# Attention in an fp32 kernel: the factors of the states' softmax go from a diagonal matrix onto the softmax matrix itself

## The chip, the cores and the metric

The kernel runs on one core of a Trainium2 chip. The metric is device time in microseconds (us), the median of several executions. One further execution was recorded by the hardware profiler, with each instruction's start and length on TensorE (PE; its weight loads are PEld), VectorE (DVE), ScalarE (ACT), GpSimd (POOL) and the DMA queues; SyncE (SP) issues most of the DMAs.

## The reference

Three stages follow one another: an attention between 512 tokens and 32 states for each of 4 batches and 8 heads, a dense layer with the mish activation, and a layer in which each token goes through one of 8 experts. Only the attention is edited:

```python
scores = scale * np.matmul(x, state.transpose(0, 1, 3, 2))      # B, H, 512, 32
a = np.exp(scores - scores.max(-1, keepdims=True))
a /= a.sum(-1, keepdims=True) + 1e-09
xread = np.matmul(a, state)
scores2 = scale * np.matmul(state, x.transpose(0, 1, 3, 2))     # B, H, 32, 512
a2 = np.exp(scores2 - scores2.max(-1, keepdims=True))
a2 /= a2.sum(-1, keepdims=True) + 1e-09
sread = np.matmul(a2, x)
out = np.concatenate([xread, sread], axis=2)                    # then the dense layer and the experts
```

## The kernel before

**Attention.** The function `attention` works in eight units, two per batch, each with four heads, so that 4 x 32 states fill the 128 partitions. Unit `u` passes four steps, one loop round apart: in round `t` the program writes `s1(t)`, `s2(t - 1)`, `s3(t - 2)` and `s4(t - 3)`.

- `s1` turns the tokens (`xt`, evacuated as `xT`), multiplies with the states (`sc`) and copies the scores out (`ss`).
- `s2` makes both softmaxes. The one over the states goes over GpSimd: `a` is the score minus its maximum `mx` (L336), ScalarE's exponential, and the product with the reciprocals `sm` (L351). For the one over the tokens TensorE turns the scores (`sb`), VectorE takes the maximum `mb`, ScalarE writes the exponential `a2` and its sums `sbs` in one instruction (L346), and VectorE makes the reciprocals of `sbs` (L353). These are one factor per row of `a2`. L355 spreads them on the diagonal of a 128 x 128 matrix, `dg`.
- `s3` turns `a` with four plain turns (`at`, L368) and brings `a2` to its turned form `a2t` by four fp32 matmuls with `dg` (L366), which apply the factors on the way; ScalarE copies `a2t` out as `a2T` (L371).
- `s4` multiplies the tokens with `a2T` (`sr`, L385); VectorE copies the result out (`XS`).

**Beside it.** From the first round on, `convert_w` turns the weights of the dense layer, 32 pieces that arrive in a 64-bit format, into pairs of reduced-precision matrices (`wih` and `wil`, `woh` and `wol`). Each piece passes GpSimd (L100), ScalarE (L97, L74), VectorE twice (L71) and GpSimd again (L75). Only two raw pieces fit (`w`), so the next load waits for a conversion.

**Dense layer.** For chunk `c` of 512 tokens and slice `f` of 128 hidden units `product` gives `m`, which is split into `mh` and `ml`; `l1` gives `h`; `mish_a` and `mish_b` are ScalarE and VectorE work on `h`; `g_split` gives `gh` and `gl`; `l2` adds into `acc`. Every product is three matmuls (`mm3`, L106 to L108). `split_x` splits the attention's result into `xh` and `xl`, for one half of a chunk with GpSimd (L75). The first rounds of the dense layer already run in the attention's last rounds.

**Experts.** A plan on VectorE and TensorE (`po`, L649) gives `perm`; with it GpSimd gathers tiles of tokens (`xg`, L884), TensorE turns them (`gt`, L889), multiplies with two weight matrices (`hp`, then, after a turn `ht` at L915, `y`), and GpSimd scatters the result (`ys`).

**The order.** No order is written out for all this up to the last tiles of the experts. A scheduler sorts the instructions of each engine from its own estimates of how long each takes, within the data dependences and the buffers. The changed program was scheduled anew.

The lines the change touches in `s3`:

```python
if n:
    T.matmul(o[:, js], d[key][:, js], d["dg"], start=True, stop=True)
else:
    T.transpose(o[:, js], d[key][:, js], ident)
```

Of the kernel before, what the change touches and what calls it, by code (L numbers as in the profile page):

```python
# [8 lines left out]
F32 = mybir.dt.float32  # L9
# [6 lines left out]
ALU = mybir.AluOpType  # L16
# [5 lines left out]
P = 128  # L22
# [30 lines left out]
def body(tc, x, state, w_in, w_out, ee, tau, w1, w2, out):  # L53
    nc = tc.nc
    T, V, A, G, Y = nc.tensor, nc.vector, nc.scalar, nc.gpsimd, nc.sync
    stack = ExitStack()

    def pool(name, bufs=1, **kw):
        return tc.tile_pool(name=name, bufs=bufs, **kw)

    def tsc(o, i, s1, op0, s2=None, op1=None):
        if op1 is None:
            V.tensor_scalar(out=o, in0=i, scalar1=s1, scalar2=None, op0=op0)  # L63
        else:
            V.tensor_scalar(out=o, in0=i, scalar1=s1, scalar2=s2, op0=op0, op1=op1)
# [7 lines left out]
    def split(hi, lo, src, eng=None):  # L73
        A.activation(hi, src, AF.Copy)  # L74
        (eng or V).tensor_tensor(out=lo, in0=src, in1=hi.bitcast(F32), op=ALU.subtract)  # L75
# [34 lines left out]
    with stack:  # L110
# [16 lines left out]
        ident = const.tile([P, P], F32, name="ident")  # L127
# [110 lines left out]
        def f32r(n, i, name):  # L238

            return xpool.tile([P, 512], F32R, tag=f"x{n}{i}", name=name)  # L240
# [25 lines left out]
        def attention(meanwhile):  # L266
            pa = ExitStack()
            tmp = pa.enter_context(pool("pa"))
# [21 lines left out]
            for h in range(4):  # L290
                q, r = divmod(h, 2)
                hs = slice(h * NST, (h + 1) * NST)
                o = SBD[hs, :, q, r * D : (r + 1) * D]
# [34 lines left out]
            def s2(u):  # L328
                d = ns[u]
                ss = d["ss"]  # L330
                v = ss.rearrange("p (g n) -> p g n", n=NST)
                mx = tmp.tile([P, 16], F32, tag="mx", bufs=2, name=f"mx{u}")
                V.tensor_reduce(mx, v, axis=AX, op=ALU.max)
                a = tmp.tile([P, 512], F32, tag="a", bufs=2, name=f"a{u}")
                av = a.rearrange("p (g n) -> p g n", n=NST)
                G.tensor_tensor(out=av, in0=v, in1=mx.unsqueeze(2).to_broadcast([P, 16, NST]), op=ALU.subtract)  # L336
                o = ps.tile([P, 512], F32, tag="acc", bufs=4, name=f"sb{u}")
                for j in range(KT):
                    T.transpose(o[:, j * P : (j + 1) * P], ss[:, j * P : (j + 1) * P], ident)
                A.activation(a, a, AF.Exp, scale=SCALE)  # L340
                mb = tmp.tile([P, 1], F32, tag="mb", bufs=2, name=f"mb{u}")
                V.tensor_reduce(mb, o, axis=AX, op=ALU.max)
                tsc(mb, mb, -SCALE, ALU.mult)
                a2 = tmp.tile([P, 512], F32, tag="a2", bufs=2, name=f"a2{u}")
                sb = tmp.tile([P, 1], F32, tag="sb", bufs=2, name=f"sbs{u}")
                A.activation(a2, o, AF.Exp, scale=SCALE, bias=mb, accum_out=sb)  # L346
                sm = tmp.tile([P, 16], F32, tag="sm", bufs=2, name=f"sm{u}")
                V.tensor_reduce(sm, av, axis=AX, op=ALU.add)
                tsc(sm, sm, 1e-9, ALU.add)
                V.reciprocal(sm, sm)  # L350
                G.tensor_tensor(out=av, in0=av, in1=sm.unsqueeze(2).to_broadcast([P, 16, NST]), op=ALU.mult)  # L351
                tsc(sb, sb, 1e-9, ALU.add)
                V.reciprocal(sb, sb)  # L353
                dg = tmp.tile([P, P], F32, tag="dg", bufs=2, name=f"dg{u}")
                tsc(dg, ident, sb, ALU.mult)  # L355
                d.update(a=a, a2=a2, dg=dg)

            def s3(u):
                d = ns[u]
                for n, key in enumerate(("a", "a2")):  # L360
                    o = ps.tile([P, 512], F32, tag="acc", bufs=4, name=f"{key}t{u}")
                    for j in range(KT):
                        js = slice(j * P, (j + 1) * P)
                        if n:

                            T.matmul(o[:, js], d[key][:, js], d["dg"], start=True, stop=True)  # L366
                        else:
                            T.transpose(o[:, js], d[key][:, js], ident)  # L368
                    if n:
                        t = d["a2T"] = tmp.tile([P, 512], F32, tag="a2T", bufs=2, name=f"a2T{u}")  # L370
                        A.activation(t, o, AF.Copy)  # L371
                    else:
                        if u < 2:
                            xh[0, u], xl[0, u] = f32r("h", u, f"xh0{u}"), f32r("l", u, f"xl0{u}")
                            split(xh[0, u], xl[0, u], o)
                        A.activation(AT[u // 2][:, u % 2, :], o, AF.Copy)
# [21 lines left out]
            for t in range(NU + 3):  # L398
                if t == 4:
                    load(3)  # L400
                if t < NU:
                    s1(t)
                if 0 <= t - 1 < NU:
                    s2(t - 1)
                if 0 <= t - 2 < NU:
                    s3(t - 2)
                if 0 <= t - 3 < NU:
                    s4(t - 3)
                for _ in range(t > 0):
                    if len(order) > len(order0) - FIRST:  # L410
                        convert_w()
                if t == 4:
                    embeddings(tmp)
                meanwhile(t)
# [725 lines left out]
```

## Time and profile before

| | us |
|---|---|
| timed runs: median of 3 (lowest, highest) | 734.07 (734.06, 740.17) |
| the profiled execution | 730.14 |
| its span, first to last instruction | 728.4 |

A profile shows one execution. A row of a timeline has the start and the length of an instruction or of several alike ones, the engine, the line of the kernel, what was written from what, and in square brackets the engine's idle time ahead of it with the releaser. Starts are counted from the start of the span. [...] Matmuls overlap, so the spacing of their starts tells more than their lengths.

### The profile page before, as it was taken

Reading aid. Unit: us, or ns where it says so; the run is one execution under the profiler, and the core shown is the slowest. Engines: PE = TensorE matmul, PEld = TensorE weight load, DVE = VectorE, ACT = ScalarE, POOL = GpSimd, SP = SyncE. Lnnn points to the kernel's source line nnn. Section 1 sums busy time; section 2 is a strip of 40 time slices with the busy share of each in tenths; the row PEclk is TensorE's granted clock in tenths of the full one; section 3 lists DMA queues with packets and bytes.
Section 4 is the critical chain, followed back from the end, with each engine's and each line's share of the span. In section 5 each row is a group of like instructions: output and inputs, shape, how many; then the busy total and the mean of one; then the engine's idle time right before and its main releaser. Section 6 shows DMA issues by size and latency. Waiting matters only on the chain.

```text
span 728.4 us, 11317 instructions
## 1 busy us (share of the span) xinstructions
PE 693.2 (95%) x3681; PEld 581.1 (80%) x3681; DVE 476.0 (65%) x981; ACT 452.6 (62%) x782; POOL 194.3 (27%) x165
## 2 busy tenths in 40 slices
PE   8888989899999999999999988799999999999994
PEld 8788868788888888888887867677888888888883
DVE  5987899998576865665667984573444752257741
ACT  5876988888697777666776776613434641246640
POOL 2785455462000210300002264212111312123101
PEclk9999999999999999999999999799999999999999
DMA  8552142340010100001000167304415631257530
GB/s 196 153 160 88 59 144 91 126 145 16 1 58 0 59 1 1 0 1 59 15 0 1 50 195 223 113 30 174 153 51 180 249 132 58 76 197 251 191 133 17
DMA packets 45499, 70.12 MB, mean 96 GB/s; under 512 B 23402, under 2 KB 23402, under 8 KB 45428
## 3 DMA queue, kind: packets, MB, share of 16 engines
q1 hardware_dynamic: 42068, 59.29, 25.3%
q0 software_dynamic: 3360, 9.99, 4.2%
q8 instruction: 31, 0.51, 0.3%
q14 instruction: 40, 0.33, 0.1%
HBM read 60.33 MB, written 9.98 MB: 97 GB/s over the span
## 4 chain that ended last, share of the span: by engine, by line
PE 45%; issue 25%; DMA 12%; DVE 9%; ACT 4%; POOL 3%; SPq 2%; POOLq 0%; DVEq 0%; ACTq 0%
DMA out<-ys,ix 7%; PE acc L106 7%; PE acc L107 7%; PE acc L108 7%; PE h L106 4%; PE h L107 4%; PE h L108 4%; DMA es<-in_moe_w 2%; DMA w<-in_moe_w_in 2%; PE m L106 2%; PE m L107 2%; PE m L108 2%; PE lg L557 1%; SPq L285 1%; PE y L108 1%
## 5 line engine op out<-in xcount | busy, mean ns | idle before, releaser
L106 PE MATMUL acc<-woh,gh 128*128 128x512 f32 x272 | 109.2, 406 | 2.3 <-ACT gh L74 2.2
L107 PE MATMUL acc<-wol,gh 128*128 128x512 f32 x272 | 109.5, 404 | 0.0
L108 PE MATMUL acc<-woh,gl 128*128 128x512 f32 x272 | 96.1, 400 | 0.0
L931 POOL DMA_INDIRECT out<-ys,ix x21 | 21.1, 1007 | 194.7 <-DVE ys L63 187.2
L477 DVE TENSOR_TENSOR er<-er 128x512 f32<-128x512 f32 x68 | 53.3, 784 | 29.1 <-ACT er L475 29.0
L106 PE MATMUL y<-w2h,hth 128*128 128x512 f32 x168 | 68.0, 404 | 0.8 <-ACTq L872 0.8
L106 PE MATMUL hp<-w1h,xth 128*128 128x512 f32 x168 | 68.5, 408 | 0.0
L475 ACT ACTIVATE er<-h,mb__103 128x512 f32<-128x512 f32 x68 | 46.5, 684 | 34.0 <-PE h L108 32.0
L108 PE MATMUL hp<-w1h,xtl 128*128 128x512 f32 x168 | 66.9, 399 | 0.0
L107 PE MATMUL hp<-w1l,xth 128*128 128x512 f32 x168 | 66.8, 398 | 0.0
L107 PE MATMUL y<-w2l,hth 128*128 128x512 f32 x168 | 66.5, 396 | 0.4 <-DVEq L872 0.4
L108 PE MATMUL y<-w2h,htl 128*128 128x512 f32 x168 | 66.7, 397 | 0.0
L106 PEld LDWEIGHTS acc<-woh,gh 128*128 128x128 f32 x272 | 52.0, 192 | 14.4 <-ACT gh L74 2.8
L74 ACT ACTIVATE hth<-ht 128x512 fp32r<-128x512 f32 x42 | 23.0, 595 | 64.3 <-PE ht L915 61.2
L107 PEld LDWEIGHTS acc<-wol,gh 128*128 128x128 f32 x272 | 52.3, 192 | 11.2
L108 PEld LDWEIGHTS acc<-woh,gl 128*128 128x128 f32 x272 | 51.2, 190 | 11.9 <-DVE gl L75 0.5
L74 ACT ACTIVATE xth<-gt 128x512 fp32r<-128x512 f32 x21 | 12.4, 595 | 75.2 <-PE gt L889 75.2
L500 ACT ACTIVATE h<-er,mb__103 128x512 f32<-128x512 f32 x68 | 47.1, 694 | 12.6 <-DVE er L477 10.4
L107 PE MATMUL h<-xl,mh 128*128 128x512 f32 x128 | 50.5, 395 | 2.5 <-POOL xl L75 2.5
L106 PE MATMUL h<-xh,mh 128*128 128x512 f32 x128 | 51.1, 399 | 0.0
L108 PE MATMUL h<-xh,ml 128*128 128x512 f32 x128 | 50.3, 393 | 0.0
L501 ACT ACTIVATE er<-er,mb__103 128x512 f32<-128x512 f32 x68 | 49.2, 723 | 1.4
(434 smaller groups left out, 1689.7 us busy)
## 6 DMA issues: line engine op xcount, KB each, us to landing
sg<-in_moe_w SPq DMA_DIRECT2D x48, 512.0 KB
w<-in_moe_w_in SPq DMA_DIRECT2D x16, 512.0 KB, 3.9
w<-in_moe_w_out SPq DMA_DIRECT2D x16, 512.0 KB, 3.2
es<-in_moe_w SPq DMA_DIRECT2D x32, 256.0 KB, 3.3
xn<-in_x SPq DMA_DIRECT2D x32, 128.0 KB, 3.6
x1d<-x SPq DMA_DIRECT2D x13, 256.0 KB, 3.3
x1d<-part SPq DMA_DIRECT2D x4, 256.0 KB
xg<-x1d,perm POOLq DMA_INDIRECT x21, 4.4
```

The costliest lines, as they stand in the source:

```text
L74: A.activation(hi, src, AF.Copy)
L106: T.matmul(o, lh, rh, start=first, stop=False)
L107: T.matmul(o, lh, rl, start=False, stop=False)
L108: T.matmul(o, ll, rh, start=False, stop=last)
L285: Y.dma_start(XN[b][:, g, :, r * D : (r + 1) * D], src[g, r])
L475: A.activation(z, h, AF.Tanh, scale=0.5, bias=mb_[:, 0:1])
L477: V.tensor_tensor(out=z, in0=z, in1=z, op=ALU.mult)
L500: A.activation(r, z, AF.Square, scale=QS, bias=mb_[:, 1:2])
L501: A.activation(z, z, AF.Square, scale=QS, bias=mb_[:, 2:3])
L557: T.matmul(o[:, j], xt[:, k * P : (k + 1) * P], enT[:, k, :].unsqueeze(1).to_broadcast([P, 8, NE]), start=k == 0, stop=k == KT - 1)
L931: G.indirect_dma_start(out=out[:, :], out_offset=bass.IndirectOffsetOnAxis(ap=ix, axis=0), in_=y, in_offset=None, bounds_check=NTOK - 1, o ...
```

## The change

The reciprocals of the sums are no longer put on a diagonal. VectorE multiplies them, one factor per row, onto the exponential `a2` in place (128 x 512 instead of 128 x 128 elements), and `a2` is turned as `a` is, by four plain turns. The tile `dg` goes; all other lines stay.

```diff
@@ s2
                 tsc(sb, sb, 1e-9, ALU.add)
                 V.reciprocal(sb, sb)
-                dg = tmp.tile([P, P], F32, tag="dg", bufs=2, name=f"dg{u}")
-                tsc(dg, ident, sb, ALU.mult)
-                d.update(a=a, a2=a2, dg=dg)
+                tsc(a2, a2, sb, ALU.mult)
+                d.update(a=a, a2=a2)
@@ s3
                     for j in range(KT):
                         js = slice(j * P, (j + 1) * P)
-                        if n:
-
-                            T.matmul(o[:, js], d[key][:, js], d["dg"], start=True, stop=True)
-                        else:
-                            T.transpose(o[:, js], d[key][:, js], ident)
+                        T.transpose(o[:, js], d[key][:, js], ident)
```

Since the program is scheduled anew, instructions also change places. Lines behind L354 have a number lower by one, behind L366 by five in the changed program. In the rows below, the number after a name is that of a buffer.

VectorE in the sixth unit, with the row that makes `dg`, before:

```order
L63 TENSOR_SCALAR sbs_804<-sbs_804 128x1
L63 TENSOR_SCALAR sm_806<-sm_806 128x16
L353 RECIPROCAL sbs_804<-sbs_804 128x1
L350 RECIPROCAL sm_806<-sm_806 128x16
L63 TENSOR_SCALAR dg_813<-ident,sbs_804 128x128
L71 SCALAR_TENSOR_TENSOR wc07x<-wc07x,w_846 128x512
```

and in the changed program, where `a_798` is the exponential `a2` of this unit:

```order
L63 TENSOR_SCALAR sbs_799<-sbs_799 128x1
L63 TENSOR_SCALAR sm_801<-sm_801 128x16
L353 RECIPROCAL sbs_799<-sbs_799 128x1
L350 RECIPROCAL sm_801<-sm_801 128x16
L63 TENSOR_SCALAR a_798<-a_798,sbs_799 128x512
L333 TENSOR_REDUCE mx_867<-ss_783 128x16
```

The scaling stands where `dg` was made; behind it the next unit's maximum now comes ahead of the weight conversion.

GpSimd at the end of the dense layer's first chunk, where it converts weights and splits the attention's result for chunk 1 (`xl`), before:

```order
L75 TENSOR_TENSOR wol_1105<-wc17x,woh_1104 128x512
L100 TENSOR_SCALAR w_1443<-w_1443 128x512
L75 TENSOR_TENSOR xl_1429<-at_154,xh_1428 128x512
L75 TENSOR_TENSOR wil_178<-wc08x,wih_170 128x512
L100 TENSOR_SCALAR w_1501<-w_1501 128x512
```

and in the changed program:

```order
L75 TENSOR_TENSOR wol_1097<-wc17x,woh_1096 128x512
L75 TENSOR_TENSOR xl_1421<-at_154,xh_1420 128x512
L100 TENSOR_SCALAR w_1435<-w_1435 128x512
L100 TENSOR_SCALAR w_1493<-w_1493 128x512
L75 TENSOR_TENSOR wil_178<-wc08x,wih_170 128x512
```

The split `xl` now stands ahead of the first of two conversions that wait for their loads.

TensorE at the plan of the experts, from the last product `po` on, before:

```order
L649 MATMUL po<-ph_4871,Q 128x44
L108 MATMUL y_5151<-w2h_5117,htl_5136 128x512
L106 MATMUL y_5151<-w2h_5117,hth_5134 128x512
L107 MATMUL y_5151<-w2l_5118,hth_5134 128x512
L108 MATMUL y_5151<-w2h_5117,htl_5136 128x512
L106 MATMUL y_5151<-w2h_5123,hth_5134 128x512
L107 MATMUL y_5151<-w2l_5124,hth_5134 128x512
L108 MATMUL y_5151<-w2h_5123,htl_5136 128x512
L106 MATMUL y_5151<-w2h_5123,hth_5134 128x512
L107 MATMUL y_5151<-w2l_5124,hth_5134 128x512
L108 MATMUL y_5151<-w2h_5123,htl_5136 128x512
L106 MATMUL hp_5233<-w1h_4803,xth_4757 128x512
```

There follow the other eleven matmuls of this `hp`, then the turn `gt` of the gathered tile. In the changed program the last rows ahead of that turn are:

```order
L108 MATMUL y_5143<-w2h_5109,htl_5128 128x512
L106 MATMUL y_5143<-w2h_5109,hth_5126 128x512
L107 MATMUL y_5143<-w2l_5110,hth_5126 128x512
L108 MATMUL y_5143<-w2h_5109,htl_5128 128x512
L106 MATMUL y_5143<-w2h_5115,hth_5126 128x512
L107 MATMUL y_5143<-w2l_5116,hth_5126 128x512
L108 MATMUL y_5143<-w2h_5115,htl_5128 128x512
L106 MATMUL y_5143<-w2h_5115,hth_5126 128x512
L107 MATMUL y_5143<-w2l_5116,hth_5126 128x512
L108 MATMUL y_5143<-w2h_5115,htl_5128 128x512
L858 UNCONDITIONAL_BRANCH
L884 MATMUL gt_5251<-ident,xg_5121 128x128 x4
```

Four more rows of `y` stand between the last `po` and these; all of `hp` stands ahead of `po`. So 22 matmuls lay between `po` and `gt` before, and 14 do now.

## Rows read from the trace of the kernel before

**Rows 1.** The page: span, and busy time of the engines (us, share, instructions).
```profile
span 728.4 us, 11317 instructions
...
PE 693.2 (95%) x3681; PEld 581.1 (80%) x3681; DVE 476.0 (65%) x981; ACT 452.6 (62%) x782; POOL 194.3 (27%) x165
```

**Rows 2.** Stretches: length, busy us of each engine, granted clock, DMA share, GB/s.
```profile
20.00:30.00 10.00, 7.44 (x66) 6.90 (x63) 9.48 (x25) 8.95 (x22) 7.35 (x8) 1.00 0.59 160
...
60.00:70.00 10.00, 8.86 (x71) 8.48 (x71) 7.30 (x21) 6.73 (x12) 5.01 (x6) 1.00 0.31 107
...
120.00:130.00 10.00, 7.92 (x40) 6.13 (x38) 10.00 (x14) 7.50 (x14) 4.21 (x4) 1.00 0.33 105
150.00:200.00 50.00, 50.00 (x240) 41.30 (x239) 40.62 (x60) 39.82 (x71) 13.37 (x13) 1.00 0.12 43
```

**Rows 3.** The chain of waits in order of time, 15 to 80 us: its pieces of `dg`.
```profile
154 pieces in order of time: start us, us, what
...
25.67 0.20 DVE dg L63
...
43.68 0.16 DVE dg L63
...
52.45 1.20 DVE dg L63
```

**Rows 4.** Timeline, TensorE: four plain turns, then a state product through `dg`.
```profile
18.63 0.61 PE L368 MATMUL at<-ident,a 128*128 128x128 f32 x4
...
19.07 1.06 PE L366 MATMUL a2t<-dg,a 128*128 128x128 f32 x8
```

**Rows 5.** VectorE: `dg` (ns min/median/max), and groups by line (busy us, mean ns).
```profile
L63 DVE TENSOR_SCALAR dg<-ident,sbs x8: 232/280/1200, 17.0 to 65.4; 128x128 f32<-128x128 f32 x8
...
L294 DVE COPY SBD<-stc 32x512 f32<-32x512 f32 x2 | 0.8, 420 | 0.1
...
L63 DVE TENSOR_SCALAR ys<-y,gt 128x512 f32<-128x512 f32 x21 | 15.7, 748 | 49.3 <-PE y L108 49.3
```

**Rows 6.** Timeline, GpSimd and VectorE around the longest `dg`.
```profile
52.30 1.27 POOL L75 TENSOR_TENSOR wil<-wc06x,wih 128x512 fp32r<-128x512 f32 x1
52.45 1.20 DVE L63 TENSOR_SCALAR dg<-ident,sbs 128x128 f32<-128x128 f32 x1
```

**Rows 7.** TensorE's waits, 12 to 75 us, then 75 to 131 us (us, times, longest).
```profile
PE sb L339 <- ACT ss L325: 4.1, 3, 2.6
...
PE h L107 <- POOL xl L75: 2.5, 1, 2.5
PE acc L106 <- ACT gh L74: 2.2, 1, 2.2
```

**Rows 8.** Stretches of 2 us behind those two waits, columns as in Rows 2.
```profile
110.00:112.00 2.00, 2.00 (x8) 1.59 (x7) 2.00 (x2) 1.60 (x3) 1.92 (x2) 0.63 0.00 0
112.00:114.00 2.00, 2.00 (x6) 1.59 (x5) 2.00 (x4) 0.83 (x2) 1.52 (x2) 0.51 0.51 123
...
132.00:134.00 2.00, 2.00 (x7) 1.52 (x6) 1.70 (x3) 1.89 (x4) 0.64 (x1) 0.50 0.51 186
```

**Rows 9.** Timeline, GpSimd, then TensorE and ScalarE's release at the two waits.
```profile
106.78 0.65 POOL L100 TENSOR_SCALAR w<-w 128x512 uint32<-128x512 uint16 x1 [1.34 <-DMA w<-in_moe_w_in]
107.50 1.77 POOL L75 TENSOR_TENSOR xl<-at,xh 128x512 fp32r<-128x512 f32 x1
...
109.33 0.50 PE L107 MATMUL h<-xl,mh 128*128 128x512 f32 x1 [2.53 <-POOL xl L75]
...
130.19 0.50 PE L106 MATMUL acc<-woh,gh 128*128 128x512 f32 x1 [2.16 <-ACT gh L74]
```

**Rows 10.** Timeline at the plan of the experts: TensorE and GpSimd.
```profile
492.38 0.60 PE L649 MATMUL po<-ph,Q 128*128 128x44 bf16 x17
...
494.41 0.98 POOL L884 DMA_INDIRECT xg<-x1d,perm  x1 [6.26 <-issue]
...
498.04 0.60 PE L889 MATMUL gt<-ident,xg 128*128 128x128 f32 x4
499.81 1.15 PE L915 MATMUL ht<-ident,h 128*128 128x128 f32 x8 [1.18 <-ACT h L908]
```

## The prediction

> **What bounds the kernel now.** I read the page first: span 728.4 us, TensorE busy for 693.2 us of it, VectorE for 476.0 [rows 1]. Then the stretches, because the edit lies in the attention alone, in the first 75 us. From 150 us on TensorE is busy in the whole of a stretch and VectorE is not (the last of [rows 2]); ahead of that it is the other way round. From 20 to 30 us VectorE works 9.48 of 10 us and TensorE 7.44; from 120 to 130 us VectorE works all of 10.00 and TensorE 7.92; only from 60 to 70 us does VectorE have air (7.30). So there is a first part, to about 130 us, in which the element engines set the pace, and a long second part in which TensorE does. A microsecond lost or won at the hand-over is carried to the end, and a microsecond of TensorE work that is saved before the hand-over is worth nothing unless TensorE sets the pace there.
>
> Next the chain of waits in order of time between 15 and 80 us: 154 pieces of VectorE, GpSimd, ScalarE and weight loads, and no TensorE piece among them. Three of the eight multiplications that make the diagonal matrix `dg` are on it [rows 3]: at 25.67, 43.68 and 52.45 us. The waits say the same from the other side: TensorE's largest wait in the attention is for ScalarE's `ss` (4.1 us in three) [rows 7]. Behind the attention it stops twice more: 2.5 us for GpSimd's `xl` and 2.2 us for ScalarE's `gh`. [...]
>
> **The change, part by part.**
>
> *TensorE.* A state product through `dg` is four matmuls of fp32, which the trace counts as eight and which take 1.06 us; four plain turns take 0.61 us in the row just ahead [rows 4]. Eight units save 8 x 0.45 = 3.6 us of TensorE's work. No TensorE piece is on the chain there, so I take 0; the bound on the good side is -3.6.
>
> *VectorE.* The product with 128 columns (median 0.28 us, 0.23 to 1.20) [rows 5] becomes one with 512, in place. The trace has no such instruction at full width. From below, the nearest is a copy from SBUF to SBUF with 512 columns, also with one source, at 0.42 us; from above, the scaling of an expert's output, the same operation with a per-row factor, but read from PSUM, at 0.75 us [rows 5]. I take 0.42, since operands in SBUF are what the new instruction has. That is +0.14 a unit, 1.1 us for eight; with the upper price 8 x 0.47 = 3.8. Three of eight are on the chain, and VectorE still has idle time around 60 us to take up lateness of the others, so I count 3 x 0.14 = +0.4, bounds 0 and +3.8. The new instruction also needs the exponential `a2` finished, but its factor `sbs` comes from that same instruction's sum, so no new wait arises; the four turns that need the scaled matrix stand a whole unit later, as the product through `dg` did. What queues behind it on VectorE is the next weight conversion or the next unit's maxima.
>
> *GpSimd beside VectorE.* One `dg` took 1.20 us: it began at 52.45, while GpSimd worked from 52.30 for 1.27 us, and both ended within 0.1 us of each other [rows 6]. [...]
>
> *The order.* The program is scheduled anew from its estimates of each instruction, so rows move on TensorE, VectorE, ScalarE and GpSimd in the first third of the program and once more at the plan of the experts, although nothing was edited there. Two places I price.
>
> First, GpSimd near 107 us. Before, the split `xl` of chunk 1 stands behind a conversion that waits for its weights: `w` at 106.78, then `xl` from 107.50 for 1.77 us [rows 9], and TensorE waits 2.53 us for it, until 109.33 [rows 9]. In the change `xl` stands ahead of that conversion. The stop and its low clock (2 x (1 - 0.63) + 2 x (1 - 0.51) = 1.7 us) could go: -4.2 us. But VectorE has no idle time from 120 to 130 us [rows 2], and TensorE's next long stop, 2.16 us for `gh` until 130.19 [rows 9], hangs on what VectorE does last before `gh`; a TensorE that comes earlier only waits longer there. I take 0, with -4.2 as bound.
>
> Second, the plan of the experts. Between the plan's last product `po`, which ends at 492.98, and the turn `gt` of the gathered tile at 498.04 [rows 10] TensorE has 22 matmuls, so 5.06 / 22 = 0.23 us each; in the change 14 stand there. The gather `xg`, which `po` releases, has 8 x 0.23 = 1.8 us less cover. It is issued at 494.41 and has landed by 498.04, since `gt` does not wait. If it landed at the last moment, `gt` waits 1.8 us; in return the 1.18 us that `ht` waits for the activation of the third tile go, because all of that tile's `hp` products now come before. Net +0.7, bounds -1.2 (the gather lands early and the wait goes) and +1.8 (the wait comes and the other stays).
>
> *Sum.* Against the profiled execution: 728.4 + 0.4 + 0 + 0 + 0.7 = 729.5 us of span. Its own time is 730.14, so 1.74 lie around the span: 731.2. The median of the timed runs is 734.07, 3.9 above the profiled execution, so on that scale the forecast is 734.07 + 1.1 = **735.2 us**.
>
> **The rivals.**
>
> *A: TensorE comes to count.* The stop for `xl` goes and VectorE, through the new order, is not late at `gh`: -4.2 + 0.7 = -3.5, 730.6 us. For it: the row on GpSimd's order is plain. Against it: VectorE is full from 120 to 130 us. That the saved 3.6 us of TensorE work show instead gives nearly the same, 734.07 - 3.6 + 0.7 = 731.2. Were the stop for `gh` avoided too, with 1.0 us of low clock in its 2 us stretch, it is 2.53 + 1.7 + 2.16 + 1.0 = 7.4 us, 726.7 us; that needs everything at once.
>
> *B: every scaling is on the path at the upper price.* +3.8 + 1.8 = +5.6, 739.7 us. For it: once the chain has turned to VectorE in a unit, each instruction there counts. Against it: three of eight on the chain, and the idle time near 60 us.
>
> [...]
>
> *D: the change does not show.* The chain's three units find their 0.14 us in other idle time and the gather lands early: 734.07 us.
>
> **How the numbers follow.** Forecast, including D, which lies within its spread: 0.60; A 0.26, of which 0.04 is the case with everything at once; B 0.09; C 0.05. The time is that of the likeliest, 735.2. The range runs from A with the one stop alone, 734.07 - 4.2 = 729.9, to B, 739.7; outside are C, the extreme of A and about a tenth more for orders that fall out otherwise. About 1% of this kernel, 7.3 us, is what a measurement can tell from no change. Faster by more than that needs the extreme of A (0.04), slower needs C and a part of B with a bad order (0.07); the rest is within 1%: 0.89.
>
> **What would show it.** [...] Weight loads for the state product should fall from 64 to 32. TensorE's idle time up to 80 us should grow by about what its work shrinks; if it doesn't, A is at work. The 2.5 us wait for `xl` should be gone, and the wait for `gh` or another of VectorE's results should have grown by as much. At the plan `gt` should wait up to 1.8 us for `xg`, and `ht` no longer for `h`. The forecast is wrong if the last stop of TensorE ahead of 150 us ends more than 3 us from where it ends now (130.19), as the hand-over then moved by more than the terms above.

## The result: 1.4% slower, and the profile after

The changed kernel takes 743.61 us (median of 11; 741.31 to 751.41) against 734.06 us for the kernel before on the same chip (median of 11). The ratio is 1.0142, with a 95% interval from 1.0115 to 1.0170: slower. The medians lie 9.5 us apart; 1.42% are 10.4 us. The forecast was 735.2 us with a range up to 739.7. It was wrong.

The page of the changed kernel, span and TensorE:

```profile
span 741.5 us, 11257 instructions
...
PE 697.7 (94%) x3649; PEld 583.5 (79%) x3649; DVE 481.7 (65%) x981; ACT 451.6 (61%) x782; POOL 192.7 (26%) x165
```

The span grew by 13.1 us, TensorE's busy time by 4.5, though TensorE has 32 passes fewer [rows 1]. So TensorE worked slower somewhere, and waited more. The stretches of [rows 2], after, and the one from 30 to 40 us (length, busy us of each engine, granted clock as a share of full speed, DMA share, GB/s):

```profile
20.00:30.00 10.00, 7.27 (x39) 7.04 (x37) 8.89 (x19) 6.88 (x15) 7.83 (x7) 0.64 0.68 180
30.00:40.00 10.00, 10.00 (x64) 9.96 (x65) 8.23 (x19) 6.36 (x15) 4.89 (x5) 0.68 0.16 51
60.00:70.00 10.00, 7.45 (x46) 6.95 (x46) 9.37 (x17) 7.04 (x12) 7.82 (x8) 0.83 0.32 107
120.00:130.00 10.00, 9.12 (x43) 7.01 (x44) 9.80 (x15) 8.82 (x17) 5.13 (x5) 1.00 0.32 105
150.00:200.00 50.00, 45.60 (x218) 37.11 (x217) 43.52 (x62) 41.18 (x73) 14.99 (x15) 1.00 0.15 54
```

Two things are new. First, the granted clock is 0.64 and 0.68 in the attention where it was 1.00; from 30 to 40 us TensorE is busy all the time and the other engines are not, with the loads nearly at rest (DMA share 0.16). Second, from 150 to 200 us TensorE is busy for 45.60 us of 50, where it had been busy for all 50: the hand-over from the element engines to TensorE has moved behind 150 us. TensorE's waits from 75 to 200 us (us in total, times, longest), and the timeline rows of the longest:

```profile
PE acc L106 <- ACT gh L74: 6.8, 3, 3.1
PE m L106 <- DVE ml L75: 1.9, 2, 1.5
PE h L107 <- POOL xl L75: 1.2, 1, 1.2
```

```profile
134.59 0.50 PE L106 MATMUL acc<-woh,gh 128*128 128x512 f32 x1 [3.12 <-ACT gh L74]
...
160.62 0.50 PE L106 MATMUL acc<-woh,gh 128*128 128x512 f32 x1 [2.92 <-ACT gh L74]
```

The wait for `xl` shrank from 2.5 to 1.2 us, and the wait for ScalarE's `gh` grew from 2.2 to 6.8 [rows 7].

Where does the time go? Take the start of ScalarE's first activation `er` of each step of the dense layer (a step is one slice `f` of one chunk, counted from 0; step 12 is slice 4 of chunk 1), after minus before, both from the span's start. The kernels of the last eight rows are those of the experiments below.

| lateness in us at step | 8 | 10 | 12 | 14 | 16 | 40 |
|---|---|---|---|---|---|---|
| start in the kernel before | 114.2 | 123.6 | 136.2 | 146.1 | 156.1 | 276.8 |
| changed kernel | 1.6 | 3.4 | **8.1** | 8.5 | 9.4 | 9.6 |
| o1: new operations, old order | 4.2 | 5.2 | 4.5 | 4.2 | 4.9 | 4.9 |
| p2: old operations, new order behind the attention | -3.3 | -1.5 | **3.1** | 3.7 | 5.8 | 6.1 |
| q4: the same, GpSimd in old order | 2.9 | 2.8 | **8.3** | 9.1 | 12.3 | 12.6 |
| r1: three engines in new order at steps 12 to 14 | -1.6 | -0.8 | **2.5** | 3.3 | 5.1 | 5.4 |
| r3: ScalarE and VectorE alone there | 1.7 | 1.7 | **5.7** | 6.4 | 8.4 | 8.6 |
| r5: TensorE alone there | 0.2 | 0.2 | 1.7 | 1.4 | 2.6 | 2.4 |
| r2: changed kernel, steps 12 to 14 in old order | -1.4 | 0.4 | 1.6 | 1.3 | **6.0** | 5.7 |
| s1: changed kernel, old order from step 12 on | 2.3 | 3.2 | 4.3 | 4.2 | 5.0 | 5.3 |

In the changed kernel about 3 us are there by step 10, and nearly 5 more arise between steps 10 and 12, in code that nobody edited. Behind step 40 the span grows by 3.5 us more; 1.57 of them are a wait at the plan of the experts (shown near the end), and the rest is not traced here.

Each row is one execution, and that of the kernel before was one of its fastest (730.14 us against a median of 734.07). So a lateness of some 2.4 us at step 40 means no loss: r5 has it, and its time is that of the kernel before.

### The profile page after: what moved, and what is told of

The parts are those of the page before. It is cut to its first block, busy times and chain, and to the rows that moved or that the text cites. A ratio compares the mean times of both kernels' runs of the same rounds, so it can differ in the third digit from the quotient of the medians.

```text
span 741.5 us, 11257 instructions
## 1 busy us (share of the span) xinstructions
PE 697.7 (94%) x3649; PEld 583.5 (79%) x3649; DVE 481.7 (65%) x981; ACT 451.6 (61%) x782; POOL 192.7 (26%) x165
## 4 chain that ended last, share of the span: by engine, by line
PE 45%; issue 25%; DMA 14%; DVE 6%; ACT 6%; POOL 2%; SPq 2%; POOLq 0%; DVEq 0%; ACTq 0%
DMA out<-ys,ix 8%; PE acc L106 7%; PE acc L107 7%; PE acc L108 7%; PE h L106 4%; PE h L108 4%; PE h L107 4%; DMA w<-in_moe_w_in 2%; PE m L106 2%; DMA w<-in_moe_w_out 2%; PE m L107 2%; PE m L108 2%; SPq L285 2%; DMA es<-in_moe_w 1%; PE lg L552 1%
## 5 line engine op out<-in xcount | busy, mean ns | idle before, releaser
L108 PE MATMUL acc<-woh,gl 128*128 128x512 f32 x272 | 98.2, 399 | 0.0
L495 ACT ACTIVATE h<-er,mb__103 128x512 f32<-128x512 f32 x68 | 47.2, 696 | 16.0 <-DVE er L472 13.1
```

Of the source, the lines that this page charges most:

```text
L108: T.matmul(o, ll, rh, start=False, stop=last)
L495: A.activation(r, z, AF.Square, scale=QS, bias=mb_[:, 1:2])
```

## The experiments: the operations apart from their order

**The tool.** An edit of one unit's arithmetic came with a new order on all engines, so the two had to be taken apart. The kernels below carry a list of numbers for each engine, the places of its instructions as the program writes them in the order wanted, and chain the instructions by edges that ask for that order and for no wait:

```diff
+ORDER = {"PE": "0-30 46-68 30-31 34-35 ...", "DVE": "...", "Activation": "...", "Pool": "...", "SP": "..."}
+def pin(tc):
+    ...
+    for k in range(a, b):
+        if was is not None:
+            tc.add_manual_dep(mine[k], was.name, mybir.DependencyInfo(mybir.DependencyClass.NoSync, ...), reason="order")
+        was = mine[k]
@@ ahead of the last tiles of the experts
+        pin(tc)
```

The kernel before and the changed one have the same number of instructions on each engine, in the same places of the program, so either can be held in the order of the other. The list as such costs nothing that shows: p3 and r5 below, the kernel before with a list that differs from its own order in one small place, take 0.9999 and 1.0003 of its time. Theories: **the operations** cost the time (the wider scaling, or the plain turns), or **the order** does.

**o1, new operations in the old order** (edit: the change, and the list of before).

> The changed arithmetic (scaling in place, four plain turns), with the instructions of every engine held in the order of the kernel before by a list of numbers at the end of the file. If the new order is what costs the time (order theory), this is the kernel before to within 2 us, 732 to 736 us, the granted clock from 20 to 40 us stays 1.00 and TensorE's last stop before 150 us ends near 130. If the operations themselves cost it (operations theory: without the products through dg TensorE falls to its lower clock after its stop near 20 us, or the wider scaling is late on VectorE), it is about as slow as the changed kernel, 741 to 746 us, with a granted clock near 0.65 from 20 to 40 us.

Measured: 736.45 us against 733.37, ratio 1.0048 (1.0021 to 1.0074): between the two ranges, a third of the loss. The clock fell as in the changed kernel (0.62 from 20 to 30 us), but the lateness, 4 to 5 us, is there from the attention on and grows no more.

**o2, old operations in the new order** (edit: the kernel before with the list of the changed kernel).

> The arithmetic of before (dg and products through it), held in the order of the changed kernel. Order theory: 741 to 746 us, and the granted clock falls from 20 to 40 us though the products through dg are there. Operations theory: 733 to 737 us, clock 1.00 from 20 to 40 us.

Measured: 740.16 against 733.37, ratio 1.0104 (1.0063 to 1.0145). So the order costs more than the operations, without any of the new ones. The clock was 1.00 from 20 to 40 us, so the order theory was wrong in that detail; it fell later, to 0.53 from 40 to 50 us, in a profile that is the slowest of the five executions (745.87 us).

**o3 and o4, the two new operations one by one, in the old order.** o3 keeps TensorE's work:

```diff
-                        T.transpose(o[:, js], d[key][:, js], ident)
+                        if n:
+                            T.matmul(o[:, js], d[key][:, js], ident, start=True, stop=True)
+                        else:
+                            T.transpose(o[:, js], d[key][:, js], ident)
```

> Order of before; VectorE scales the matrix in place as in the change, but TensorE keeps four fp32 products, now with the identity, so its work is that of before. If the wider scaling on VectorE is the cost: 740 us or more. If the plain turns or the order are: 734 to 736 us (my priced 0.14 us per scaling, at most 8 of them), clock 1.00 from 20 to 40 us.

Measured: 734.44 against 733.37, ratio 1.0026 (1.0000 to 1.0051). o4 keeps VectorE's work (`dg` is made and left unused) and has the plain turns:

```diff
-                        if n:
-                            T.matmul(o[:, js], d[key][:, js], d["dg"], start=True, stop=True)
-                        else:
-                            T.transpose(o[:, js], d[key][:, js], ident)
+                        T.transpose(o[:, js], d[key][:, js], ident)
```

> Order of before; dg is still made by VectorE but not used, and the matrix is turned by four plain turns, so the factors of the states' softmax are left out of the result. If plain turns in the place of products let TensorE's clock fall: 740 us or more, clock under 0.8 from 20 to 40 us. If the order or the scaling is the cost: 732 to 735 us, clock 1.00.

Measured: 736.62, ratio 1.0052 (1.0031 to 1.0073): the clock fell (0.72 from 20 to 30 us) as the first theory has it, but the time lies between the two ranges. The turns alone, which are less work for TensorE, cost as much as both operations together.

**p4, twice the turns.** Old order, scaling in place, each turn of the scaled matrix issued twice:

```diff
-                        T.transpose(o[:, js], d[key][:, js], ident)
+                        for _ in range(1 + n):
+                            T.transpose(o[:, js], d[key][:, js], ident)
```

> Order of before, scaling in place as in the change, but each of the four plain turns of the scaled matrix is issued twice into the same place, so TensorE has eight passes a unit as with the products, and all of them plain turns. If the granted clock follows how long TensorE works, it stays 1.00 from 20 to 40 us as with the identity products, 734 to 735 us. If plain turns do not hold the clock whatever their number: clock 0.6 to 0.76 from 20 to 40 us as in the two kernels with four plain turns in this order, 736 to 738 us.

Measured: 735.10 against 733.73, ratio 1.0013 (0.9999 to 1.0027). TensorE had more work than in o1, by an estimate 8 x (1.04 - 0.60) = 3.5 us (the turns of one unit at a granted clock of 1.00), and the kernel took less. The stretches from 20 to 30 and from 30 to 40 us (columns as above), first of o1:

```profile
20.00:30.00 10.00, 7.87 (x40) 7.63 (x38) 7.71 (x24) 7.64 (x18) 6.72 (x8) 0.62 0.59 161
30.00:40.00 10.00, 10.00 (x66) 10.00 (x66) 8.34 (x23) 7.77 (x16) 5.38 (x6) 0.70 0.25 74
```

of o4:

```profile
20.00:30.00 10.00, 6.49 (x35) 6.42 (x35) 8.30 (x23) 8.28 (x18) 7.28 (x7) 0.72 0.72 180
30.00:40.00 10.00, 10.00 (x72) 10.00 (x72) 8.58 (x26) 7.86 (x17) 5.80 (x6) 0.76 0.29 84
```

of p4:

```profile
20.00:30.00 10.00, 8.52 (x75) 7.97 (x73) 9.46 (x25) 8.62 (x21) 7.42 (x8) 1.00 0.65 160
30.00:40.00 10.00, 7.16 (x61) 6.60 (x62) 9.44 (x24) 7.27 (x15) 5.71 (x6) 1.00 0.53 125
```

In o1, o4 and the changed kernel, with four plain turns in place of the product, TensorE's clock falls at its stop near 21 us (in the changed kernel 0.71 from 22 to 24 us, then 0.50 until 36), and TensorE is then busy for the whole of 30 to 40 us, at 0.68 to 0.76 on the mean the slowest engine. The changed kernel shows the moment on TensorE's timeline:

```profile
20.00 0.60 PE L317 MATMUL xt<-ident,xn 128*128 128x128 f32 x4
23.33 1.12 PE L317 MATMUL xt<-ident,xn 128*128 128x128 f32 x4 [2.73 <-ACT a2T L366]
24.24 3.51 PE L380 MATMUL sr<-a2T,xn 128*128 128x64 f32 x16
```

and the kernel before the same place without a fall (1.00 from 20 to 30 us [rows 2]), behind a shorter stop:

```profile
22.51 0.66 PE L317 MATMUL xt<-ident,xn 128*128 128x128 f32 x4 [1.95 <-ACT a L346]
23.01 0.65 PE L339 MATMUL sb<-ident,ss 128*128 128x128 f32 x4
23.50 1.90 PE L385 MATMUL sr<-a2T,xn 128*128 128x64 f32 x16
```

The same sixteen matmuls `sr` take 1.90 us in the kernel before, at a granted clock of 1.00, and 3.51 us in the changed one, at 0.50. The length of the stop alone does not decide it: in o1 the stop was 2.1 us and the clock fell; in the kernel before a stop of 2.6 us for `ss` [rows 7], near 60 us, left it at 1.00. And s1 below, which has the operations and the order of the changed kernel up to there, made the same stop of 2.73 us and stayed at 1.00; its clock fell at the next stops, near 31 us.

```profile
22.96 0.66 PE L317 MATMUL xt<-ident,xn 128*128 128x128 f32 x4 [2.73 <-ACT a2T L366]
```

One profile is one execution, but the mean granted clock over the whole span is listed for every timed execution. The kernel before has between 0.9785 and 0.9795 on the mean in each of its sets (16 to 25 executions); o1 has 0.972 (9), o4 0.972 (10), s1 below, which has the four turns as well, 0.973 (10); with the products or the turns doubled, o3 has 0.977 (10) and p4 0.979 (10). The mean does not say where the clock was low, and other kernels have it nearly as low: o2, p2 and r3, which keep the products, 0.975, 0.974 and 0.975. Of the five profiles with four plain turns, four fell at 22 to 24 us and one at 32; of the fifteen others one fell at 32 us (r1) and none earlier.

**q3, more products.** The opposite of the change, on the kernel before in its own order:

```diff
-                            T.transpose(o[:, js], d[key][:, js], ident)
+                            T.matmul(o[:, js], d[key][:, js], ident, start=True, stop=True)
```

> The opposite of the change, in the order of before: not only the scaled matrix but also a is turned by four fp32 products (with the identity) in place of four plain turns, 3.6 us more work for TensorE. If plain turns are what lets TensorE's clock fall in the attention, the clock is 1.00 from 20 to 75 us and the median comes near the 730.1 us of the profiled execution of before, which had no such fall: 730 to 732 us. If not: 734 to 737 us.

Measured: 733.41 against 733.63, by the ratio 1.0021 (1.0003 to 1.0039): in neither range. The clock is 1.00 up to 60 us and 0.83 from 60 to 70, the mean of ten executions 0.983, the highest of all. It gains nothing all the same. That the added work eats up what the clock gives would explain it; no run separates the two.

## The experiments: where the order costs

**p1 and p2, the new order in halves.** Operations of before; the cut lies behind the last state product `sr` and its copy, where the sets of instructions ahead agree in both orders.

```diff
-ORDER: place 0 to the end: as before
+p1: "PE" places 0 to 415, "DVE" 0 to 166, "Activation" 0 to 92, "Pool" 0 to 47 as changed; behind them as before
+p2: the same places as before; behind them as changed
```

> Arithmetic of before. Every engine is held in the order of the changed kernel up to the end of the attention (the last state product sr and its copy), and in the order of before behind it. If the new order loses its time in the attention (lateness of weight conversions, loads later): the 6 to 8 us of the whole new order, about 740 us. If it loses them behind the attention: 733 to 735 us. If the two add up: 736 to 738 us.

> The other half: order of before up to the end of the attention, order of the changed kernel behind it, arithmetic of before. If the loss lies behind the attention: about 740 us, with TensorE waiting some 6 to 7 us for ScalarE's gh between 75 and 200 us. If it lies in the attention: 733 to 735 us and a wait for gh near the 2.2 us of before.

Measured: p1 735.52 against 733.73, ratio 1.0022 (0.9999 to 1.0044); p2 740.92, ratio 1.0111 (1.0089 to 1.0132). Most of the loss lies behind the attention, in the dense layer or later. In p2 the rows have the mark of the changed kernel, the longer wait for `gh` (75 to 200 us):

```profile
PE acc L106 <- ACT gh L74: 6.8, 3, 3.1
PE m L106 <- DVE ml L75: 2.1, 2, 1.7
```

**p3, q1, s2: GpSimd near 107 us**, the place that the prediction priced. p3 moves the split `xl` alone:

```diff
-POOL: w (107), xl, wil, w (111), wil
+POOL: xl, w (107), wil, w (111), wil
```

> The kernel before with one move: on GpSimd the split xl of chunk 1 stands ahead of the weight conversion that waits for its load near 107 us, as in the changed kernel. By my prediction TensorE's wait of 2.5 us for xl goes and only another wait grows: 733 to 735 us. If TensorE sets the pace there: 729 to 731 us. If the later conversion of the weights matters more: 736 us or more.

Measured: 734.10 against 733.73, ratio 0.9999 (0.9976 to 1.0021). No gain, as the prediction had it, but not by the way that it named. The wait for `xl` shrank to 0.45 us, and the wait for `gh` that was to grow stayed at 2.17. Right behind `xl` two new stops took part of the gain, for ScalarE's `xh` and for an earlier `gh`; where the rest went these rows do not show.

```profile
110.22 0.50 PE L107 MATMUL h<-xl,mh 128*128 128x512 f32 x1 [0.45 <-POOL xl L75]
...
111.86 0.50 PE L106 MATMUL h<-xh,mh 128*128 128x512 f32 x1 [0.90 <-ACT xh L74]
112.83 0.50 PE L106 MATMUL acc<-woh,gh 128*128 128x512 f32 x1 [0.47 <-ACT gh L74]
...
132.85 0.50 PE L106 MATMUL acc<-woh,gh 128*128 128x512 f32 x1 [2.17 <-ACT gh L74]
```

q1 takes all five instructions in the order of the changed kernel. There the split `wil` also stands behind a second conversion `w` that waits for its load. My theory by then was that this blocks GpSimd's queue, then ScalarE, then VectorE.

```diff
-POOL: w (107), xl, wil, w (111), wil
+POOL: xl, w (107), w (111), wil, wil
```

> The kernel before with five instructions of GpSimd near 107 us in the order of the changed kernel: the split xl first, then both conversions w that wait for their loads, and only then the split wil of weight 8. Blocking theory: the second conversion waits for a load that comes about 4 us later, wil stands behind it, ScalarE's next conversion waits for wil's buffer and VectorE for ScalarE, 2 us each near 113 us: 736 to 740 us, against 734 for the move of xl alone. If those 2 us of VectorE are made up before the hand-over to TensorE, or if the cost needs the other engines' new order too: 733 to 735 us.

Measured: 731.75 against 733.63, ratio 0.9966 (0.9941 to 0.9990), below both ranges. The blocking is there, and costs nothing: GpSimd waits 2.27 us for the load, ScalarE 1.81 for `wil`, and the kernel is faster if anything.

```profile
111.65 0.78 POOL L100 TENSOR_SCALAR w<-w 128x512 uint32<-128x512 uint16 x1 [2.27 <-DMA w<-in_moe_w_in]
...
113.83 0.68 ACT L97 ACTIVATE wc010x<-w 128x512 f32<-128x512 f32 x1 [1.81 <-POOL wil L75]
```

That theory fell. s2 is q1 once more, as the only kernel that was faster than both:

> The kernel before with the five instructions of GpSimd near 107 us in the order of the changed kernel, once more, with more rounds. If its gain is real: a ratio of 0.995 to 0.998 to the kernel before. If it was chance: 1.000.

Measured: 732.44 against 732.79, ratio 0.9984 (0.9958 to 1.0010). Its second interval includes 1; a gain of some 2 us is likely, not settled.

**q4, the new order behind the attention without GpSimd's part** (p2 with "Pool" wholly as before).

> As the kernel with the new order behind the attention (740.9 us), but GpSimd keeps the order of before. If GpSimd's blocked queue is what costs: 734 to 736 us. If the new order of VectorE, ScalarE and TensorE costs it: 739 to 742 us.

Measured: 743.41 against 733.63, ratio 1.0157 (1.0096 to 1.0218), four executions from 740.95 to 749.84. So it is VectorE, ScalarE or TensorE.

**q2, the new order at the plan alone** ("PE" from place 2253, "DVE" from 754, "Activation" from 605 as changed).

> The kernel before with the new order only at the plan and the first tiles of the experts, from 450 us on; all ahead of it in the order of before. My prediction priced this at +0.7 us (bounds -1.2 to +1.8): 733 to 736 us. If the 3 us and more by which the profiles with the new order fall back behind 490 us are of this place: 736 to 738 us.

Measured: 734.86 against 733.63, ratio 1.0012 (0.9986 to 1.0037): about what was forecast for this place. `gt` waits 1.57 us for the gather here too.

**r1, r3, r5: the stretch of steps 12 to 14.** All profiles with the new order behind the attention jump in lateness between steps 10 and 12 (bold in the table above). r1 puts the new order into that stretch of the kernel before, r3 for ScalarE and VectorE alone, r5 for TensorE alone:

```diff
+r1: "PE" places 652 to 685, "DVE" 242 to 266, "Activation" 184 to 217 as changed; all else as before
+r3: "DVE" and "Activation" alone        r5: "PE" alone
```

> The kernel before, with TensorE, ScalarE and VectorE in the order of the changed kernel only from about 132 to 150 us (34, 34 and 25 instructions). There ScalarE takes two weight copies and a weight's first step ahead of the first activation of step 12, VectorE two more conversion instructions, and TensorE the product m of four steps later ahead of the product h of step 12. Stretch theory: 738 to 741 us. If the loss is spread over the whole dense layer: 733 to 735 us.

> The kernel before, with ScalarE and VectorE alone in the new order of that stretch. If ScalarE's weight copies ahead of the activation of step 12 are the cause: 737 to 741 us. If TensorE's early m is: 733 to 735 us.

> The kernel before, with TensorE alone in the new order of that stretch (the twelve matmuls of m ahead of h of step 12). If TensorE's order is the cause: 736 us or more. If ScalarE's and VectorE's is: 733 to 735 us.

Measured against 732.94: r1 738.44, ratio 1.0077 (1.0050 to 1.0104); r3 739.82, ratio 1.0088 (1.0055 to 1.0122); r5 734.04, ratio 1.0003 (0.9977 to 1.0029). In r3 57 changed places, 34 on ScalarE and 23 on VectorE, cost 0.88%, 6.5 us. ScalarE's timeline in the kernel before at step 12:

```profile
136.23 0.69 ACT L475 ACTIVATE er<-h,mb__103 128x512 f32<-128x512 f32 x1 [0.76 <-PE h L108]
...
137.91 0.63 ACT L74 ACTIVATE wih<-wc014x 128x512 fp32r<-128x512 f32 x1
...
139.04 0.62 ACT L74 ACTIVATE wih<-wc015x 128x512 fp32r<-128x512 f32 x1
```

and in r3, with the end of TensorE's product `h` that `er` reads:

```profile
137.67 0.39 PE L108 MATMUL h<-xh,ml 128*128 128x512 f32 x1
...
139.15 0.60 ACT L74 ACTIVATE gh<-h 128x512 fp32r<-128x512 f32 x1 [1.10 <-DVE h L71]
140.19 0.63 ACT L74 ACTIVATE wih<-wc015x 128x512 fp32r<-128x512 f32 x1 [0.44 <-DVE wc015x L71]
141.37 0.67 ACT L97 ACTIVATE wc18x<-w 128x512 f32<-128x512 f32 x1 [0.54 <-DMA w<-in_moe_w_out]
141.94 0.68 ACT L475 ACTIVATE er<-h,mb__103 128x512 f32<-128x512 f32 x1
```

In the kernel before, `er` takes `h` as soon as it is there, and the weight conversions follow. In the new order of r3 two weight copies, the previous step's `gh` and the first instruction of a further weight stand ahead of it, each waiting for VectorE or a load (1.10, 0.44 and 0.54 us), so `h` lies ready from 138.1 until 141.94. VectorE and TensorE get the step 4 us later, and TensorE stops where it did not stop before:

```profile
149.73 0.39 PE L106 MATMUL m<-wih,STh 128*128 128x256 f32 x1 [1.90 <-DVE ml L75]
158.52 0.50 PE L106 MATMUL acc<-woh,gh 128*128 128x512 f32 x1 [2.85 <-ACT gh L74]
```

VectorE's new order points the same way: its part of step 12, `er`, stands behind the first conversion of that further weight, `wc18`, which VectorE takes up only at 142.14; in the kernel before `er` stands ahead of it.

```profile
142.14 0.69 DVE L71 SCALAR_TENSOR_TENSOR wc18x<-wc18x,w 128x512 uint32<-128x512 uint32 x1 [1.38 <-POOL w L100]
142.75 1.78 DVE L477 TENSOR_TENSOR er<-er 128x512 f32<-128x512 f32 x1
```

No run has the new order on one of the two engines alone, so their shares stay open.

In the changed kernel this makes half of the jump. The last matmul of `h` ends near 142.0, and `er` starts at 144.32, behind the same weight copy: 2.3 us. The other half is there when `h` comes. It ends 5.8 us later than in the kernel before (136.2), against 3.4 us of lateness at step 10, and the longer wait for `gh` until 134.59 lies between. First the last matmul of `h` in the kernel before, then the changed kernel:

```profile
135.81 0.39 PE L108 MATMUL h<-xh,ml 128*128 128x512 f32 x1
```

```profile
141.59 0.39 PE L108 MATMUL h<-xh,ml 128*128 128x512 f32 x1
...
143.22 0.63 ACT L74 ACTIVATE wih<-wc015x 128x512 fp32r<-128x512 f32 x1 [0.70 <-DVE wc015x L71]
143.75 0.66 ACT L97 ACTIVATE wc18x<-w 128x512 f32<-128x512 f32 x1
144.32 0.67 ACT L470 ACTIVATE er<-h,mb__103 128x512 f32<-128x512 f32 x1
```

**r2 and s1: the repair in the changed kernel.** r2 restores the old order in that stretch alone, s1 from step 12 to where both orders agree again:

```diff
+r2: "PE" places 652 to 685, "DVE" 242 to 266, "Activation" 184 to 217 as before; all else as changed
+s1: "PE" places 652 to 1157, "DVE" 242 to 360, "Activation" 184 to 324 as before; all else as changed
```

> The changed kernel as it is, with that stretch alone in the order of before. Stretch theory: the 743.6 us fall by 4 to 6 us, to 737 to 740 us. Spread theory: 742 us or more.

Measured: 743.68 against 732.94, ratio 1.0153 (1.0106 to 1.0201). No gain, by four executions that spread from 738.19 to 746.63; the profile is the fastest of them. In it the jump at step 12 is gone, and one of 4.7 us stands between steps 14 and 16, where the restored stretch ends; TensorE's stop has moved with it.

```profile
159.21 0.39 PE L106 MATMUL m<-wih,STh 128*128 128x256 f32 x1 [2.28 <-DVE ml L75]
```

> The changed kernel with TensorE, ScalarE and VectorE in the order of before from step 12 of the dense layer (about 135 us) to where both orders agree again; everything ahead of it, the attention included, GpSimd and the plan of the experts as changed. If the weight conversions that stand ahead of the activations in steps 12 to 17 are the cause: 736 to 739 us, what the new operations and the new order of the attention leave. If the loss arises ahead of step 12 and only shows there: 742 us or more.

Measured: 738.72 against 732.79, ratio 1.0074 (1.0044 to 1.0104). Half of the loss is gone, and no step jumps. What is left, 0.74%, is near the sum of o1 and p1, 0.48% and 0.22%.

**What is settled and what is open.** Settled: with the old order on TensorE, ScalarE and VectorE from step 12 on, the changed kernel loses 0.74% instead of 1.42% (about 5.0 us less; the interval of each is some 0.3% to either side). The new operations in the old order cost 0.48% (3.5 us), and the plain turns alone cost as much. That conversions ahead of activations are what costs in that order is shown for the stretch of steps 12 to 14 in the kernel before (r3, with r5 against TensorE); for the changed kernel it is read from its rows, and r2 shows that putting this stretch right moves the stop and gains nothing. The parts of the order do not add up with o1 to the whole (0.48 + 0.22 + 1.11 = 1.81%), so some lateness hides other lateness. That the turns act through the clock is borne out by three things, the clock in the profiles, the mean clock of all executions and p4; but p4's own profile lost its clock later, from 40 to 52 and near 65 us, 6.8 us of full-speed time in all, with little harm, and why the clock falls at one stop and not at a longer one stays open.

## Why the prediction was wrong, step by step

- **"No TensorE piece is on the chain there, so I take 0."** The step that failed first. It counted TensorE's saved work, 3.6 us, as worth nothing; saving it cost 3.8 us instead (o4). The work removed stood next to TensorE's stop, and without it the clock fell there in four of five profiles: the changed kernel's profile loses 8.5 us of full-speed time in the attention (the sum over stretches of 2 us of their length times what the clock lacks to 1.00), against 3.4 or 5.1 us in nine profiles of other kernels with the operations and the order of before there. And TensorE had little slack to begin with. "Only from 60 to 70 us does VectorE have air" is a misreading: from 40 to 50 us TensorE worked 9.23 us and VectorE 6.45. At a clock of 0.68 there was none, 10.00 of 10 us from 30 to 40 us in the changed kernel. The kernel before:

```profile
40.00:50.00 10.00, 9.23 (x81) 8.73 (x80) 6.45 (x17) 7.57 (x16) 8.46 (x8) 1.00 0.43 138
```

  The prediction priced low clock behind stops (0.63 and 0.51, then 0.50 [rows 8]) but looked for it only at two stops in the dense layer.
- **"Two places I price."** The second failed step, and the larger: the order cost its time at a third place, 0.68% or about 5.0 us from step 12 of the dense layer on (s1). The prediction went through the new order for what now comes earlier and asked what that gains; it did not go through the queues of ScalarE and VectorE for what now stands *in front of* the activations that TensorE waits for. Both orders were there to be read, and the hand-over was known to hang on `gh`.
- **The scaling** was sized rightly: 434, 482 and 1079 ns (shortest, median, longest) against the 0.42 us taken, with two of eight over 1 us.

```profile
L63 DVE TENSOR_SCALAR a<-a,sbs x8: 434/482/1079, 17.5 to 70.7; 128x512 f32<-128x512 f32 x8
```

  Its cost by itself, 0.26% or 1.9 us (o3; interval from 0.0 to 3.7), lies within the bounds of 0 and +3.8, above the +0.4 taken. Rival C, with a chance of 0.05, took every scaling to be held up by a GpSimd instruction and priced each from the one `dg` of 1.20 us [rows 6]: 8 x (1.20 + 0.14 - 0.28) = +8.5, 742.6 us. No run shows this; two of eight scalings are long, and that its time was the nearest is luck. In the kernel before, the next `dg` lies wholly inside a GpSimd row and took 0.27 us, so meeting one did not always mean waiting.

```profile
36.73 2.18 POOL L75 TENSOR_TENSOR wil<-wc03x,wih 128x512 fp32r<-128x512 f32 x1
37.51 0.27 DVE L63 TENSOR_SCALAR dg<-ident,sbs 128x128 f32<-128x128 f32 x1
```

- **GpSimd near 107 us** was rightly priced at 0 (p3), but the reason given, a longer wait for `gh` until 130 us, did not come: 2.17 us against 2.16.
- **The plan** was priced at +0.7, and q2 gives +0.9, from -1.0 to +2.7; but the +0.7 took the wait of `ht` as gone, and it stayed. The gather came late, as forecast as a possibility, and `ht` still waits for `h` (1.18 us as before), which is the case of the bound, +1.8. q2 cannot tell the two apart. The changed kernel:

```profile
511.00 0.63 PE L884 MATMUL gt<-ident,xg 128*128 128x128 f32 x4 [1.57 <-DMA xg<-x1d,perm]
512.81 1.15 PE L910 MATMUL ht<-ident,h 128*128 128x128 f32 x8 [1.18 <-ACT h L903]
```

- **"The median is 3.9 above the profiled execution"** was carried as a constant. It was a sign: that execution (mean clock 0.984) had no low clock in the attention at all, while each of the nine other profiles named above had. The margin that TensorE seemed to have was in part that of one lucky execution.
- **The sign named for a wrong forecast came true**: the last stop ahead of 150 us ends at 134.59 instead of 130.19, and two more follow.

The range was too narrow because its bounds were those of the edited operations, while the new order, which changed 488 places on TensorE, 268 on VectorE, 246 on ScalarE and 23 on GpSimd, was bounded by two places.

## What to carry to other kernels

Where an edit lets a scheduler sort the program anew, hold the old order and measure the two apart before explaining either; read the new order for what now stands ahead of the instructions that the bounding engine waits for, on the engines that feed it (in r3 `er` started at 141.94, though its `h` was ready at 138.1). And do not count work taken from an engine with slack as worth nothing: here four passes a unit less went with an earlier fall of TensorE's clock (0.62 to 0.72 from 20 to 30 us in four of five profiles), and in the changed kernel that made it the slowest engine for 13 us. Look at how far the profiled execution lies from the median before taking its stretches for the rule.

## What the runs showed of the hardware

- The mean clock differs between executions of one kernel, and the time with it. Over the 110 timed executions of the kernel before that stand beside the experiments, each 0.01 of mean granted clock goes with 4.0 us (correlation -0.70): 731.3 us on the mean at 0.984 and above, 734.9 at 0.972 to below 0.976.
- Four plain turns a unit went with a clock of 0.62 to 0.72 from 20 to 30 us in four profiles (the changed kernel, o1, o4 and r2) and of 1.00 in the fifth (s1); eight plain turns in the same place went with 1.00 (p4). The mean clock over all executions is 0.979 in p4 and 0.972 in o1, so here the number of the turns told, not only that they were plain.
- More work was less time: p4 gives TensorE an estimated 3.5 us more than o1 and takes 1.0013 of the time of the kernel before, o1 1.0048.
- The same stop can end either way: of two profiles with the same attention, both with a stop of 2.73 us near 21 us, the changed kernel's fell to 0.50 behind it and s1's stayed at 1.00.
